# Residual of two tiles moved from VectorE to TensorE and ScalarE, and a down product cut into two column blocks

## The chip, the cores and the metric

The kernel runs on one core of a Trainium2 chip. The metric is the device time of one execution in microseconds, the median of several runs; less is better. The profile's span, from first to last instruction, is 1.7 to 1.8 us shorter than the time of the same execution.

Names used below: PE is TensorE, DVE is VectorE, ACT is ScalarE, POOL is GpSimd, SP is SyncE. A tile is 128 of the 2048 tokens.

## The reference, cut to what matters

```python
# x: (1, 2048, 448); H = 16 heads of 28; F = 1792
x = A_x
h = x + A_ref(layernorm(x))        # linear attention: softmax features, num / den, then @ wo
h2 = h + B_ref(layernorm(h))       # (sigmoid(hn @ w_gate) * (hn @ w_up)) @ w_down
```

`num / den` is the normalisation of the attention output, tile by tile. `h = x + (o @ wo)` is the first residual; its row sums start the second layer norm. The last step multiplies with `w_down` and adds `h`.

## The kernel before

Every operation is recorded in a graph with what it reads and writes; `ORDER` fixes each engine's queue, and waits between engines are derived from the graph. So a change consists of operations and of new queue orders.

```python
def num(t):                        # attention output of tile t, then its normalisation
    b = {1: 2}.get(t, 6)           # PSUM banks 6 and 7 for every tile but tile 1
    op("pe", "num%d" % t, ...)     # 16 small matmuls
    op("dve", "rsm%d" % t, ...)    # reciprocal
    op("dve", "qq%d" % t, ...)     #   needs rsm
    op("dve", "b%d" % t, ...)      #   needs qq
    op("dve", "c%d" % t, ...)      #   needs b
    op("dve", "den%d" % t, ...)    #   needs c; last reader of the banks: num(t+1) waits for it
    op("dve", "rden%d" % t, ...)
    op(("pool", "dve"), "o%d" % t, ...)
# ...
def resid(t, b):                   # b: the bank that holds o @ wo of tile t
    op("dve", "h%d" % t, ...)      # h = psum + x, with row sums
    op("dve", "nm%d" % t, ...)     # minus mean
    op("act", "sq%d" % t, ...)     # square, with row sums
    op("pool", "ve%d" % t, ...); op("pool", "pow2_%d" % t, ...)
    op("dve", "hn%d" % t, ...)     # normalised h
    # tiles 0 and 1: four PE transposes (hT) and a VectorE copy (hTe); others: a DMA transpose
# ...
def gate_up(t0, n, ff):            # 14 blocks ff; gate and up banks (4,5) for even, (0,1) for odd ff
    op("pe", "ga" + nm, f1, r=hk + wgu_keys, ...)   # waits for the hidden tiles and eight weight loads
    op("pe", "gb" + nm, f2, ...)
    op("act", "sig" + nm, ...)     # tanh of the gate bank
    op("dve", "hh" + nm, ...)      # (tanh + 1) * up, frees the banks
# ...
def finish(t, b):
    op("dve", "fin%d" % t, ...)    # down product * 0.5 + h
    op("sp", "out%d" % t, ..., dma="out", nring=16)
# ... at the end of SyncE's queue:
if e == "sp":
    for sem, v in last_out.items():        # every DMA semaphore: loads, transposes, outputs
        eng.wait_ge(sems[sem], v)
```

`down1` does the down product of tiles 12 to 15, one tile and 448 columns at a time; tile 13 was the last to end. The changed kernel ends with tile 15.

The softmax here doesn't subtract the row's maximum and nothing guards it: scores larger than these inputs give would overflow.

Of the kernel before, what the change touches and what calls it, by code (L numbers as in the profile page):

```python
# [6 lines left out]
ALU = mybir.AluOpType  # L7
# [11 lines left out]
class Graph:  # L19
# [86 lines left out]
    def emit(self, nc):  # L106
# [71 lines left out]
P = 128  # L178
D = 448
H = 16  # L180
# [25 lines left out]
        "x1 x0 ld_k0 x2 ld_k2 x4 x6 ld_v0 x10 ld_v2 x8 ld_q2 ld_q1 ld_q3 x12 ld_q0 xT4 xT5 x14 xT6 xT7 xT8 xT9 xT10 "  # L206
        "xT11 xT12 xT13 xT14 xT15 ld_wg0 ld_wu1 ld_wu3 ld_wd1 ld_wg1 ld_woo1 ld_wg3 ld_woe1 ld_wu0 ld_woe0 ld_wg2 "
        "ld_woo0 ld_wu2 ld_wd6 ld_wd5 oT2 ld_wd2 oT3 oT4 oT5 ld_wd4 oT6 ld_wd3 ld_wd0 oT7 hT2 hT3 hT4 oT8 oT9 hT5 hT6 "
        "hT7 oT11 oT10 oT12 out3 out1 hT9 hT8 oT13 hT11 hT10 oT14 oT15 out5 hT12 hT14 out2 hT15 out4 hT13 out9 out7 "
        "out10 out6 out14 out0 out15 out12 out11 out8 out13 "  # L210
# [4 lines left out]
        "ek10 xn14 ek11 xn15 v1_11 ek12 eq0_0 ek13 v1_13 ek14 v1_14 ek15 v1_15 eq0_1 kvzB eq1_0 eq1_1 eq2_0 oT0e oT1e "  # L215
        "eq2_1 sq0 sq1 eq3_0 eq3_1 sig0_1 sig0_0 sig0_3 sig0_2 sig0_5 sig0_4 sq2 sq3 sig0_7 sig0_6 sig0_9 sig0_8 "
        "sig0_11 sig0_10 sq5 sig0_12 sig0_13 sq4 sq7 sig2_0 sig2_1 sq6 sig2_3 sig2_2 sig2_5 sig2_4 sig2_6 sig2_7 "
        "sig2_8 sig2_9 sig2_10 sig2_11 sig2_12 sig2_13 sig4_1 sq9 sig4_0 sig4_3 sq8 sig4_2 sig4_5 sig4_4 sig4_7 "
        "sig4_6 sig4_9 sq10 sig4_8 sq11 sig4_11 sig4_10 sig4_13 sig4_12 sig8_1 sig8_0 sq13 sig8_2 sig8_3 sig8_4 "
        "sig8_5 sq12 sig8_6 sq14 sq15 sig8_7 sig8_9 sig8_8 sig8_10 sig8_11 sig8_13 sig8_12 sig12_0 sig12_1 sig12_3 "  # L220
        "sig12_2 sig12_5 sig12_4 sig12_7 sig12_6 sig12_8 sig12_9 sig12_11 sig12_10 sig12_12 sig12_13 "
# [3 lines left out]
        "ppa0 warm9 ppb0 vva0 xT3 xT2 vvb0 ppa2 ppb2 vva2 vvb2 kva0 w2m1_1 w2m1_0 pva4 kvb0 pvb4 pva5 kva1 pvb5 kvb1 "  # L225
        "pva6 kva2 pvb6 pva7 w2m1_2 w2m1_3 pvb7 pva8 kvb2 kva3 pvb8 kvb3 pva9 kva4 pvb9 kvb4 pva10 kva5 pvb10 pva11 "
        "kvb5 kva6 pvb11 pqa0_0 pva12 kvb6 kva7 pvb12 kvb7 pqb0_0 kva8 pva13 kvb8 kva9 pvb13 pva14 kvb9 kva10 pvb14 "
        "kvb10 kva11 pva15 kvb11 pvb15 pqa0_1 kva12 pqb0_1 kvb12 kva13 pqa1_0 kvb13 kva14 pqb1_0 kvb14 kva15 kvb15 "
        "pqa1_1 num0 num1 pqb1_1 pqa2_0 pqb2_0 num2 pqa2_1 oT0 pqb2_1 oT1 num3 woa0 wob0 pqa3_0 num4 pqa3_1 pqb3_0 "
        "pqb3_1 num5 hT0 hT1 ga0_1 woa2 gb0_1 ga0_0 num6 gb0_0 ga0_3 wob2 gb0_3 ga0_2 gb0_2 num7 ga0_5 ga0_4 gb0_5 "  # L230
        "gb0_4 woa4 ga0_7 ga0_6 gb0_7 gb0_6 wob4 num8 ga0_9 ga0_8 gb0_9 gb0_8 ga0_11 ga0_10 gb0_11 gb0_10 woa6 num9 "
        "wob6 ga0_13 ga0_12 gb0_13 gb0_12 dn0_0 dn0_4 ga2_0 ga2_1 gb2_0 gb2_1 dn0_8 dn0_11 ga2_3 num10 ga2_2 gb2_3 "
        "dp0_0 gb2_2 dp0_4 ga2_5 ga2_4 gb2_5 gb2_4 dp0_8 dp0_11 ga2_6 ga2_7 gb2_6 gb2_7 woa8 ga2_8 ga2_9 gb2_8 gb2_9 "
# [6 lines left out]
        "dn10_8 ga12_0 ga12_1 gb12_0 dn8_0 dn10_11 gb12_1 ga12_2 dp10_0 ga12_3 dn8_4 gb12_3 gb12_2 dp10_4 dn8_8 "  # L240
        "ga12_5 dn8_11 ga12_4 gb12_5 gb12_4 dp8_0 dp8_4 ga12_7 ga12_6 gb12_7 dp10_8 dp10_11 gb12_6 dp8_8 dp8_11 "
        "ga12_9 ga12_8 gb12_9 gb12_8 dm14_0 dm12_0 dm15_0 ga12_11 ga12_10 gb12_11 gb12_10 dm12_4 dm14_4 dm13_0 "
        "ga12_12 ga12_13 gb12_12 gb12_13 dm15_4 dm14_8 dm15_8 dm12_8 dm15_10 dm14_10 dm14_12 dm14_13 dm15_12 dm12_10 "
        "dm12_12 dm15_13 dm12_13 dm13_4 dm13_8 dm13_10 dm13_12 dm13_13 "
# [3 lines left out]
        "bst10 agg11 bst9 bst7 agg6 agg7 agg9 bst8 agg8 agg10 xT3e xT2e ss0 nm1_8 nm1_6 rs0 ss1 rs1 bst12 bst13 ss2 "  # L248
        "bst14 rs2 agg14 xn8 ss3 agg13 agg12 rs3 xn9 bst15 ss4 agg15 xn10 ve1_12 ss5 rs4 ss6 rs5 ss7 rs6 v1_8 ss8 "
        "v1_9 rs7 ss9 rs8 v1_10 ss10 rs9 rs10 ss11 v1_12 rs11 phi10 ss12 rs12 ss13 rs13 ss14 rs14 ss15 rs15 phi15 "  # L250
        "kvzA kvzD kvzC rsm0 qq0 b0 rsm1 c0 qq1 den0 b1 rden0 c1 rsm2 den1 qq2 rden1 b2 c2 den2 rden2 rsm3 qq3 b3 c3 "
        "den3 rden3 h0 nm0 h1 rsm4 nm1 qq4 b4 c4 den4 hn0 hn1 rsm5 hT0e hT1e rden4 qq5 b5 c5 den5 rden5 hh0_1 rsm6 "
        "qq6 b6 hh0_0 c6 h2 den6 hh0_3 rden6 hh0_2 rsm7 h3 qq7 nm3 nm2 b7 hh0_5 hh0_4 c7 den7 rden7 o7 hh0_7 hh0_6 "
        "hn2 rsm8 hn3 qq8 h4 hh0_9 hh0_8 b8 h5 c8 den8 hh0_10 nm4 hh0_11 nm5 rsm9 h6 qq9 h7 b9 c9 hh0_12 hh0_13 nm7 "
        "rden8 nm6 den9 hh2_0 hh2_1 hn4 rsm10 rden9 qq10 b10 hh2_3 c10 hh2_2 hn6 hn7 den10 hh2_5 hh2_4 fin0 fin1 "
        "hh2_6 hh2_7 hn5 rden10 hh2_8 hh2_9 h8 h9 hh2_10 hh2_11 rsm11 qq11 nm9 b11 hh2_13 c11 hh2_12 den11 rsm12 qq12 "
        "nm8 b12 c12 rden11 hh4_1 hh4_0 o10 den12 hh4_3 rsm13 qq13 b13 rden12 hh4_2 c13 hh4_5 den13 fin3 hn9 rden13 "
        "hh4_4 hn8 fin2 rsm14 hh4_7 o13 qq14 b14 c14 hh4_6 den14 h10 h11 nm10 hh4_9 nm11 rsm15 hn10 hh4_8 hn11 hh4_11 "
        "qq15 h13 h12 hh4_10 b15 c15 hh4_13 nm13 hh4_12 den15 nm12 rden15 o15 rden14 hh8_1 hh8_0 o14 hh8_2 hh8_3 fin4 "
        "fin5 hh8_4 hh8_5 h15 h14 nm14 hh8_6 nm15 hn12 hn14 hh8_7 hh8_9 hh8_8 hn13 hn15 hh8_11 hh8_10 hh8_12 hh8_13 "  # L260
        "fin6 fin7 hh12_0 hh12_1 hh12_3 hh12_2 hh12_5 hh12_4 hh12_7 fin11 hh12_6 fin9 fin10 fin8 hh12_8 hh12_9 "
        "hh12_11 hh12_10 hh12_12 hh12_13 fin14 fin15 fin12 fin13 "
# [3 lines left out]
        "pow1_2 nb1_3 ve1_4 nm1_4 pow1_4 nb1_2 nb1_4 xn2 mask2 opad0 ve1_6 pow1_6 ve1_8 v1ones pow1_8 nb1_6 phi0 "  # L266
        "nb1_8 xn7 phi1 phi2 phi3 nm1_12 pow1_12 nb1_12 phi4 phi5 phi6 phi7 phi8 phi9 phi11 phi12 phi13 phi14 kvzones "
        "o0 o1 o2 o3 ve0 pow2_0 ve1 pow2_1 o4 o5 o6 ve2 pow2_2 ve3 pow2_3 ve5 ve4 pow2_4 o8 pow2_5 ve7 o9 ve6 pow2_7 "
        "pow2_6 ve8 ve9 o11 pow2_9 o12 pow2_8 ve10 pow2_10 ve11 pow2_11 ve12 pow2_12 ve14 pow2_14 ve15 ve13 pow2_15 "
        "pow2_13 "  # L270
# [3 lines left out]
    "pq:0,0,4 pq:0,1,4 kvz pq:1,0,0 pq:1,1,4 pq:2,0,0 num:0 num:1 ot:0 ot:1 wo:0 pq:2,1,4 pq:3,0,0 num:2 num:3 "  # L274
    "wo:2 pq:3,1,4 gu:0,2 num:4 num:5 wo:4 gu:2,2 num:6 num:7 wo:6 down:0,2 num:8 num:9 wo:8 down:2,2 num:10 "
    "num:11 wo:10 gu:4,4 num:12 num:13 wo:12 down:4,2 num:14 num:15 wo:14 down:6,2 gu:8,4 down:8,2 down:10,6 "
    "gu:12,4 down1:12,2 down1:13,3 down1:14,6 down1:15,7 "
# [31 lines left out]
def build(nc, A_x, A_wqkv, A_w_phi, A_wo, B_w_gate, B_w_up, B_w_down, out):  # L309
# [8 lines left out]
    NX, NO, NH, NPHI, NS, NE, NV, NSG, NHH = 3, 4, 3, 3, 3, 5, 5, 4, 2  # L318

    with ExitStack() as es:  # L320
# [99 lines left out]
        def kvzones(e):  # L420
            e.tensor_copy(kvz[:, 0:2, :, :].rearrange("p a g (h e) -> p a g h e", e=E)[:, :, :, :, E - 1],
                          maskK[:, :, :, 0][:, :, None, :].to_broadcast([P, 2, G, 2]))
            return e.tensor_tensor(kvz[:, 2, :, :].rearrange("p g (h e) -> p g h e", e=E)[:, :, :, E - 1],
                                   maskK[:, 0, :, 0][:, None, :].to_broadcast([P, G, 2]),
                                   maskK[:, 1, :, 0][:, None, :].to_broadcast([P, G, 2]), ALU.add)

        op("pool", "kvzones", kvzones, r=["maskK"], w=KVZ)


# [255 lines left out]
        def num(t):  # L685
            s, c = t % NS, t // 4
            b = {1: 2}.get(t, 6)

            def f(e):
                def part(half, x):  # L690
                    return [(bk(b + x)[:, (sg * G + gg) * 2 * E:(sg * G + gg + 1) * 2 * E], eq[c][half, sg, gg, TS(t)],
                             kvz[half, x if sg == x else 2, gg, :], True, True) for sg in range(2) for gg in range(G)]
                return both(e, part(QL, 0), part(QH, 1))
            op("pe", "num%d" % t, f, r=[("eq", c, i) for i in range(2)] + KVZ, w=[B(b), B(b + 1)], rows=64,
               half={b: 0, b + 1: 1})
            ov = psum[:, b * 512:(b + 2) * 512].rearrange("p (a n) -> p a n", a=2)
            OPv = ov[:, :, 0:8 * E].rearrange("p a (h e) -> p a h e", e=E)
            OMv = ov[:, :, 8 * E:16 * E].rearrange("p a (h e) -> p a h e", e=E)
            BB = [B(b), B(b + 1)]

            def h2(ap):
                return ap[:, s, :].rearrange("p (a h) -> p a h", a=2)

            def h3(ap):
                return ap[:, s, :, :].rearrange("p (a h) e -> p a h e", a=2)
# [20 lines left out]
            if t >= 2:  # L726
                otrans(t)
# [36 lines left out]
        def wout(t):  # L764
            def ot(t):
                return lambda h, k: oT[h, t % NO, k, :]
# [84 lines left out]
        for step in PROGRAM.split():  # L851
# [19 lines left out]
            elif k == "down1":  # L871
                down1(v[0], v[1], late)
# [37 lines left out]
```

## Time and profile before

| | before |
|---|---|
| time, three runs | 207.3 us (206.97 to 207.31) |
| span | 205.35 us |
| PE busy | 196.1 us, 96% |
| PE idle between 50 and 72 us | 1.8 us |
| after the last matmul | 4.4 us |

The prediction below shows the lines and how to read them: which engine is full, where TensorE is not, and what each of its gaps waited for. One view the prediction quotes only in words. The source view of SyncE's final waits in the kernel before (line, engine, operation, count, shortest/median/longest duration in ns, first and last start in us):

```profile
L174 SPq EVENT_SEMAPHORE  x48: 17/28/28, 202.0 to 204.9; - x48
```

48 wait instructions in 2.9 us stand between the last output's issue and the end.

### The profile page before, as it was taken

The numbers are of one execution on the slowest core, as the hardware profiler recorded it, in microseconds if no ns is written. First come the engines' busy times: TensorE is split into PE (matmuls) and PEld (weight loads), VectorE is DVE, ScalarE is ACT, GpSimd is POOL, SyncE is SP. The second block draws the span as 40 slices with busy tenths as digits, with TensorE's granted clock in tenths as the row PEclk, the third lists the DMA queues.
The fourth block names the chain that finished last, engine by engine and source line by source line (L and its number), as shares of the span: only waits on it lengthen the run. The fifth ranks groups of instructions, "written<-read, shape, count | busy, mean of one in ns | idle before, by whom it ended". The sixth has DMA issues, their size and how long they took to land.

```text
span 205.4 us, 5793 instructions
## 1 busy us (share of the span) xinstructions
PE 196.1 (96%) x2456; PEld 108.7 (53%) x2456; DVE 135.8 (66%) x341; ACT 96.2 (47%) x189; POOL 60.4 (29%) x101
## 2 busy tenths in 40 slices
PE   7899999989989999999999999999999999999991
PEld 2745556655566676676444444445555545544450
DVE  5899999879899996776758886356232523353151
ACT  2889999879782636222342532335322122132100
POOL 4699998963443304400041110001400000000000
PEclk9999999999999999999999999999999999999999
DMA  5975653999314630412006311110321000020013
GB/s 151 314 139 121 81 80 54 330 287 282 96 30 96 144 56 0 80 34 46 3 0 123 78 30 25 30 26 24 78 51 26 0 0 3 0 89 3 0 40 117
DMA packets 32722, 16.25 MB, mean 79 GB/s; under 512 B 24952, under 2 KB 31800, under 8 KB 32696
## 3 DMA queue, kind: packets, MB, share of 16 engines
q1 hardware_dynamic: 32192, 15.86, 33.2%
q8 instruction: 19, 0.31, 0.6%
q10 hardware_dynamic: 504, 0.03, 0.2%
q14 instruction: 7, 0.06, 0.1%
HBM read 8.34 MB, written 1.84 MB: 50 GB/s over the span
## 4 chain that ended last, share of the span: by engine, by line
PE 88%; DVE 7%; DMA 1%; issue 1%; ACT 0%; POOL 0%; DVEq 0%
PE psum L292 82%; PE psum L836 5%; DVE st L493 2%; DMA x_sb<-in_A_x_dram 1%; PE psum L561 1%; DVE b_sb L709 1%; DVE c_sb L712 1%; PE psum L486 1%; DVE kvz L677 1%; DVE x_sb L740 1%; DVE xnT L479 0%; DVE mv L494 0%; DVE hn_pad L754 0%; DVE x_sb L843 0%; DVE rsm L706 0%
## 5 line engine op out<-in xcount | busy, mean ns | idle before, releaser
L292 PE MATMUL psum<-xnT,wg_sb 64*128 64x512 bf16 (+1 forms) x490 | 94.3, 334 | 1.2 <-DVE hhT L810 0.6
L292 PE MATMUL psum<-xnT,wu_sb 64*128 64x512 bf16 (+1 forms) x490 | 94.3, 334 | 0.1
L809 ACT ACTIVATE sg_sb<-psum 128x512 bf16<-128x512 f32 (+1 forms) x70 | 34.9, 511 | 88.6 <-PE psum L292 88.0
L810 DVE SCALAR_TENSOR_TENSOR hhT<-sg_sb,psum 128x512 bf16<-128x512 bf16 (+1 forms) x70 | 39.1, 577 | 50.9 <-ACT sg_sb L809 50.3
L292 PEld LDWEIGHTS psum<-xnT,wg_sb 64*128 64x128 bf16 x490 | 43.9, 94 | 24.6 <-DVE hhT L810 5.8
L292 PEld LDWEIGHTS psum<-xnT,wu_sb 64*128 64x128 bf16 x490 | 43.9, 94 | 14.2 <-PE psum L292 0.3
L292 PE MATMUL psum<-wd_sb,hhT 64*128 64x448 bf16 x336 | 37.2, 349 | 0.0
L292 PEld LDWEIGHTS psum<-wd_sb,hhT 64*128 64x128 bf16 x336 | 17.0, 94 | 15.0 <-DVE x_sb L740 0.6
L616 POOL TENSOR_TENSOR phi<-hhT,rs 128x896 bf16<-128x896 bf16 x14 | 24.0, 1735 | 0.9 <-PE psum L292 0.8
L292 PE MATMUL psum<-Wk,xnT 64*128 64x448 bf16 x112 | 22.3, 350 | 0.3
L292 PE MATMUL psum<-wv_sb,xnT 64*128 64x448 bf16 x112 | 22.4, 351 | 0.1
L748 POOL TENSOR_SCALAR ve<-ssq 128x1 f32<-128x1 f32 x16 | 3.4, 215 | 64.5 <-ACT junk L745 64.0
L612 DVE TENSOR_REDUCE ss<-hhT 128x32 f32<-128x896 bf16 x16 | 17.0, 1062 | 0.7 <-ACT hhT L609 0.6
L292 PE MATMUL psum<-xnT,Wq 64*120 64x512 bf16 x112 | 14.7, 383 | 0.1
L722 POOL TENSOR_TENSOR o_pad<-c_sb,rden 128x448 bf16<-128x448 bf16 x11 | 10.3, 936 | 14.6 <-DVE rden L717 12.7
L292 PE MATMUL psum<-wo_e,oT 64*128 64x448 bf16 x56 | 13.2, 350 | 0.3 <-ACT oT L479 0.3
L292 PE MATMUL psum<-wo_o,oT 64*128 64x448 bf16 x56 | 13.2, 350 | 0.1
L745 ACT ACTIVATE junk<-x_sb,nm 128x448 bf16<-128x448 bf16 x16 | 10.6, 663 | 2.7 <-DVE nm L743 2.7
L843 DVE SCALAR_TENSOR_TENSOR x_sb<-psum,x_sb 128x448 bf16<-128x448 f32 x16 | 9.4, 619 | 3.5 <-PE psum L836 3.1
L836 PE MATMUL psum<-wd_sb,hhT 128*128 128x448 bf16 x56 | 11.1, 353 | 0.0
L292 PEld LDWEIGHTS psum<-Wk,xnT 64*128 64x128 bf16 x112 | 7.6, 94 | 5.4 <-ACT hhT L609 0.7
L493 DVE BATCH_NORM_STATS2 st<-x_sb 128x6 f32<-128x448 bf16 x16 | 9.3, 609 | 1.6 <-DMA x_sb<-in_A_x_dram 1.5
(82 smaller groups left out, 238.0 us busy)
## 6 DMA issues: line engine op xcount, KB each, us to landing
out_dram<-x_sb SPq DMA_DIRECT2D x16, 112.0 KB, 1.8
x_sb<-in_A_x_dram SPq DMA_DIRECT2D x7, 224.0 KB, 4.5
wd_sb<-in_B_w_down_dram SPq DMA_DIRECT2D x7, 224.0 KB, 4.4
wg_sb<-in_B_w_gate_dram SPq DMA_DIRECT2D x3, 448.0 KB, 7.9
wu_sb<-in_B_w_up_dram SPq DMA_DIRECT2D x3, 448.0 KB, 7.0
wv_sb<-in_A_wqkv_dram SPq DMA_DIRECT2D x2, 224.0 KB, 5.0
wk_sb<-in_A_wqkv_dram SPq DMA_DIRECT2D x2, 196.0 KB, 3.7
wo_e<-in_A_wo_dram SPq DMA_DIRECT2D x1, 336.0 KB, 9.0
```

The costliest lines, as they stand in the source:

```text
L292: p = e.matmul(o, lhsT=w, rhs=r, start=st, stop=sp, tile_position=(row, 0))
L486: p = e.transpose(ps[:, kt * P:(kt + 1) * P], src, ident[:])
L493: op("dve", "bst%d" % t, lambda e: e.bn_stats(st1[:, t, :], x_sb[:, t, :]), r=[("x", t)], w=[("st1", t)])
L612: op("dve", "ss%d" % t, lambda e: e.tensor_reduce(ss[:, s, :], eks, AX.X, ALU.add), r=[("ek", s)], w=[("ss", s)])
L616: return e.tensor_tensor(phi[:, sp, :, :, :].rearrange("p b a n -> p (b a) n")[:, :, 0:56].rearrange("p b (h d) -> p b h d", h=2), eks.rea ...
L722: return e.tensor_tensor(o_pad[:, so, off:off + D].rearrange("p (h d) -> p h d", h=H), c_sb[:, s, :, 0:DH], rden[:, s, :][:, :, None].to_b ...
L745: op("act", "sq%d" % t, lambda e: e.activation(junk[:, t % 2, :], h_sb[:, t, :], ACT.Square, bias=nm2[:, t:t + 1], accum_out=ssq2[:, t:t + ...
L748: op("pool", "ve%d" % t, lambda e: e.tensor_scalar(ve2[:, t:t + 1], ssq2[:, t:t + 1], 1.0 / D, EPS, op0=ALU.mult, op1=ALU.add), r=[("ssq2" ...
L809: op("act", "sig" + nm, lambda e: e.activation(sg_sb[:, k, 0:N], bk(bg)[:, 0:N], ACT.Tanh, scale=0.5), r=[B(bg)], w=[("sg", k)])
L810: op("dve", "hh" + nm, lambda e: e.scalar_tensor_tensor(out=hhT[(t0 // 4) % NHH][:, ff, ns], in0=sg_sb[:, k, 0:N], scalar=1.0, in1=bk(bu)[ ...
L836: p = e.matmul(bk(b)[:, 0:D], lhsT=hb[:, ff, TS(t)], rhs=wd_sb[:, ff, :], start=ff == 0, stop=ff == FT - 1)
L843: op("dve", "fin%d" % t, lambda e: e.scalar_tensor_tensor(out=h_sb[:, t, :], in0=bk(b)[:, 0:D], scalar=0.5, in1=h_sb[:, t, :], op0=ALU.mul ...
```

## The change

Its intent: VectorE is over 90% busy between 50 and 72 us, so the first two tiles' residual is added by identity matmuls into the same PSUM bank as the projection, and evacuated on ScalarE with row sums. The last tile's down product is cut into 320 and 128 columns, so that only a small evacuation and a small output follow the last matmul. With this come a copy (oT1) moved from ScalarE to VectorE, o7 moved to POOL (and o8 and o9, later on, from POOL to VectorE), a fourth buffer for the normalisation, mask columns moved from POOL to ScalarE, and new queue orders on all engines. The core of the diff:

```diff
-        def resid(t, b):
+        def resid(t, b, ha=False):
+            if ha:
+                op("act", "h%d" % t, lambda e: e.activation(h_sb[:, t, :], bk(b)[:, 0:D], ACT.Identity, accum_out=sum2[:, t:t + 1]), ...)
+            else:
                 op("dve", "h%d" % t, ...)
@@ def wout(t):
+            ha = t in (0,)
+            def xp(t, b, h, first):
+                return [(bk(b)[:, 0:D], ident[h, :], x_sb[h, t, :], first, False)] if ha else []
-                return both(e, [(bk(2)...
+                return both(e, xp(t, 2, LO, True) + [(bk(2)...
@@ def down1
-        def down1(t, b, parts):
+        def down1(t, b, parts, w=0):
+            for nm, b, lo, hi in (("dm", b, 0, D - w), ("dl", 4, D - w, D))[:1 + (w > 0)]:
+                ...                       # matmuls, evacuation and output of columns lo to hi
@@ PROGRAM
-    "... down1:14,6 down1:15,7 "
+    "... down1:14,6 down1:15,7,128 "
@@ ORDER, "sp": the weight loads
-  ld_wg0 ld_wu1 ld_wu3 ld_wd1 ld_wg1 ld_woo1 ld_wg3 ld_woe1 ld_wu0 ld_woe0 ld_wg2 ld_woo0 ld_wu2 ld_wd6 ld_wd5 oT2 ...
+  ld_wg0 ld_wu1 ld_wu3 ld_wd1 ld_wg1 ld_woe0 ld_wu0 ld_woe1 ld_woo0 ld_woo1 ld_wg3 ld_wg2 ld_wd6 ld_wd2 ... ld_wu2 oT2 ...
@@ ORDER, "dve": the first tiles
-  ... den3 rden3 h0 nm0 h1 rsm4 nm1 qq4 b4 c4 den4 hn0 hn1 rsm5 hT0e hT1e rden4 qq5 b5 c5 den5 rden5 hh0_1 ...
+  ... den2 oT1e rsm3 ... rden2 rden3 rsm4 nm1 qq4 b4 nm0 c4 den4 rden4 hn1 rsm5 qq5 b5 hn0 c5 hT1e den5 hT0e rden5 ...
@@ ORDER, "pe": the first gate/up blocks
-  ... num5 hT0 hT1 ga0_1 woa2 gb0_1 ga0_0 num6 gb0_0 ga0_3 wob2 ... ga0_9 ga0_8 gb0_9 gb0_8 ga0_11 ...
+  ... num5 pqb3_1 hT1 hT0 num6 ga0_1 ga0_0 gb0_1 gb0_0 woa2 num7 ... ga0_9 ga0_8 gb0_9 gb0_8 woa6 ga0_11 ...
```

## The prediction

> **What bounds the kernel now.** I read the page first, then the chain of work that ended last, then busy time by stretch, then the timelines of TensorE, VectorE and ScalarE between 50 and 72 us, and last the final 10 us. The page's part 1:
>
> ```profile
> PE 196.1 (96%) x2456; PEld 108.7 (53%) x2456; DVE 135.8 (66%) x341; ACT 96.2 (47%) x189; POOL 60.4 (29%) x101
> ```
>
> TensorE is busy 96% of a 205.4 us span, so 9.3 us without a matmul is all there is to win unless matmul work goes away. Busy time by stretch (us, then PE, PEld, DVE, ACT, POOL busy with counts) says where those 9.3 us lie:
>
> ```profile
> 50.00:60.00 10.00, 8.82 (x127) 4.99 (x125) 9.19 (x31) 8.71 (x14) 4.97 (x9) 1.00 0.40 97
> 60.00:72.00 12.00, 11.36 (x208) 8.03 (x204) 11.27 (x39) 5.67 (x15) 4.17 (x7) 1.00 0.48 104
> 72.00:183.00 111.00, 110.95 (x1298) 60.36 (x1300) 64.83 (x163) 36.01 (x78) 12.24 (x28) 1.00 0.17 34
> 201.00:205.40 4.40, 0.00 (x0) 0.00 (x0) 0.62 (x1) 0.00 (x0) 0.00 (x0) 1.00 0.30 102
> ```
>
> From 72 to 183 us TensorE loses 0.05 us: nothing the change does there can matter except through the matmul count. Idle time sits in 50 to 72 (1.18 + 0.64 = 1.8 us), in the last 4.4 us, and before 50, where the change barely reaches. In 50 to 72 VectorE is at 92% and 94%: this is the one long stretch where TensorE is fed by a full VectorE. The chain of waits for 50 to 60 us agrees: from 52.23 to 59.28 it runs on VectorE through num3's and num4's normalisation, h0, h1, the two layer-norm outputs and the transposes' copies. TensorE's own rows (start, us, what, idle before and releaser):
>
> ```profile
> 52.53 0.36 PE L292 MATMUL psum<-wo_e,oT 64*128 64x448 bf16 x1 [0.34 <-ACT oT L479]
> 57.74 0.40 PE L292 MATMUL psum<-kvz,eq 56*128 56x60 bf16 x16 [0.19 <-DVE den L714]
> 59.37 0.27 PE L292 MATMUL psum<-xnT,wg_sb 64*128 64x256 bf16 x1 [0.58 <-DVE xnT L479]
> 72.04 0.28 PE L292 MATMUL psum<-xnT,wg_sb 64*128 64x256 bf16 x1 [0.61 <-DVE hhT L810]
> ```
>
> These four gaps add up to 1.72 us. The first is the wait for the copy of oT1, the third for the normalised first tiles; the last is a bank being freed: gb0_9 ends, tanh 0.38 us, product 0.42 us, and no other matmul had been placed between.
>
> The VectorE work that the change takes away, and the end of the kernel:
>
> ```profile
> 54.46 0.56 DVE L740 SCALAR_TENSOR_TENSOR x_sb<-psum,x_sb 128x448 bf16<-128x448 f32 x1
> 55.13 0.62 DVE L740 SCALAR_TENSOR_TENSOR x_sb<-psum,x_sb 128x448 bf16<-128x448 f32 x1
> 200.99 0.63 DVE L843 SCALAR_TENSOR_TENSOR x_sb<-psum,x_sb 128x448 bf16<-128x448 f32 x1 [0.92 <-PE psum L836]
> ```
>
> **What the Trainium skill says.** "TensorE: Matmul & The Clock Gate", Back-to-back issue gap, gives N/2.4 + 2.5 ns between isolated warm matmuls: 189 ns for 448 columns. The trace agrees: the output projection's pairs start at 52.73, 52.92, 53.11. "ScalarE: Activation LUTs", What ACT_TABLE_LOAD costs, gives 186 ns + 0.833 ns per element with immediate operands (an estimate of 559 ns for 448), about 93 ns more with a pointer bias; the trace has 0.54 us for a 448 copy from PSUM and 0.66 to 0.67 us for the Square with bias, which is followed by a 0.19 us accumulator read. "PSUM — Partial Sum Buffer", The four PSUM rules, says that a nonzero seed for an accumulation should go through TensorE as an identity matmul, or be added after evacuation; the change goes from the second form to the first. No run yet shows its cost. "VectorE: DVE Perf Modes", The TRN2 errata, gives (120 + FD)/0.96 ns for a PSUM source: 592 ns at 448; the trace has 0.56 to 0.63 us.
>
> **The change part by part.**
>
> *Residual of tiles 0 and 1.* It removes h0 and h1 from VectorE: from 54.46 to the next operation at 55.06 is 0.60, from 55.13 to 55.67 another 0.54, so 1.14 us. It adds four half-array identity matmuls of 448 columns, two concurrent pairs at 0.19: 0.38 us of TensorE, all inside the chain from oT1 to the residual. On ScalarE it adds two evacuations with an accumulator: starts of such a copy lie 0.43 us apart (rows at 40.46 and 40.88), plus about 0.16 for the read, 0.6 each, so 1.2 us. Before, h on VectorE and the squares on ScalarE overlapped; now h1, h0, sq1, sq0 follow each other on one engine.
>
> *oT1's copy goes from ScalarE to VectorE.* It costs VectorE 0.38 (the two hT copies take 0.76). Before, oT1 was ready at 51.85, the copy ended at about 52.48, the projection started at 52.53. VectorE is free at 51.7 once rden2 is put later, so I expect the projection at 52.34: 0.2 us earlier.
>
> *o7 moves to POOL* (VectorE minus 0.55), and the mask columns go from POOL to ScalarE. The latter ended at 44.17 before and the masks waited for matmuls until 44.62, so it gives nothing. VectorE's balance up to 72 us: -1.14 + 0.38 - 0.55 = -1.3 us.
>
> *The order.* Every pair of gate/up blocks of the first half chunk now has a filler behind it; woa6 stands where the 0.61 gap was. That gap's true cost is 71.16 to 72.04 less the 0.11 pitch, 0.77 us.
>
> *Last tile in blocks of 320 and 128.* 14 matmuls at 0.190 become 14 at about 0.137 and 14 at about 0.060 (the 128-column transposes start 0.06 apart): 2.66 becomes 2.76, +0.10. The last evacuation shrinks from 0.63 to an estimated 0.29 (a 256-column one takes 0.41, a 512 one 0.69, so 1.1 ns per column): -0.34. What comes after is fixed: the last output is issued at 201.64 and lands at 203.32, but SyncE then runs 48 wait instructions, first at 202.0, last at 204.9, about 61 ns each. The landing is hidden beneath them, so a smaller last transfer gains nothing by being small; one more output semaphore adds up to 0.06. Tail: +0.10 - 0.34 + 0.06 = -0.18 us.
>
> *The middle, walked through by hand.* Projection from 52.34 over nine pairs instead of seven to results at 54.45. ScalarE: h1 from 54.5, h0 55.1, sq1 55.7, sq0 56.4 to 57.15; POOL's two small steps take 0.8 each: scales at 57.3 and 58.1. VectorE interleaves num4 and num5: hn1 57.35, hn0 58.8 (it stands after b5 in the queue), hT1 copied at 60.2, hT0 at 60.75. Gate/up then starts near 60.8 instead of 59.37, with num6 (0.24) already done. That is 1.2 us late, 0.38 of it the added matmuls. Then it is given back: the projection of tiles 2 and 3 no longer lies between the first gate/up blocks, VectorE's load is lower, and the 0.77 gap closes. At ga0_13, where both orders have done the same work, I get 75.5 against 75.14: +0.36 us. My walk is conservative with VectorE (I let it idle about 1.2 us in all), so the true value may lie a microsecond lower.
>
> **The rivals.**
> 1. *VectorE was the limit and the relief comes through* (for: 92 to 94% busy where TensorE waits; against: num to normalisation to num is a round trip that fewer operations only turn into idle time). The middle gains 1.3 - 0.38 = 0.9 us, the tail 0.2: 206.2.
> 2. *ScalarE's serial chain takes VectorE's place* (for: ScalarE is at 8.71 of 10 us in 50 to 60 and the q exponentials that free banks 4 and 5 come after; my walk). Middle +0.36, tail -0.18: 207.5.
> 3. *Late loads*: one up-weight load moves behind five down-weight loads. It landed at 52.7; five loads of 224 KB at the 280 to 330 GB/s of that stretch take 3.4 to 4 us and put it near 56.5, still before 59. Nothing; if it came in late, 208.5.
> 4. *The tail gains more*, if the landing and not SyncE's waits were the limit: another 0.3. The landing 1.6 us before the last wait speaks against it.
>
> **Range and chances.** I give rival 1 somewhat more weight than my walk, as the new order was evidently arranged around the freed VectorE: 0.55 x 206.2 + 0.4 x 207.5 + 0.05 x 208.5 = 206.8. The range takes in both with a few tenths for the runs' own spread (206.97 to 207.31): 205.6 to 208.1. Faster by 2% would need 203.1, thus 4.1 us, when the gaps in reach total 1.8 plus about 0.3 of tail: 2 in 100. Slower by 2% would need a new stall of 4 us: 2 in 100.
>
> **What would show it right or wrong.** Right: two VectorE rows of L740's kind fewer, two ScalarE evacuations of 448 with accumulator reads at about 54.5; the two output-projection groups still at 56 matmuls each, and 4 more with the identity; projection start near 52.3; no gap of 0.6 near 72; last evacuation near 0.29 us, then the same row of waits on SyncE. Wrong: gate/up starting before 59.5 would mean that my chain of h1, h0, sq1, sq0 is too pessimistic, and the time goes to 206 or under; a gap before it above 2 us, or TensorE waiting for the q exponentials at its second gate/up block, puts it above 207.5. A tail after the last matmul other than about 4.1 us would say that SyncE's waits are not what follows it.

## The result, and the profile after

| | before | after |
|---|---|---|
| median of 4 runs, us | 207.31 (206.97 to 207.35) | 207.04 (206.96 to 207.22) |
| ratio, 95% interval | | 0.9992 (0.9975 to 1.0009) |

A ratio here is the mean time of one kernel's runs over the mean of the other's in the same rounds, so it is not quite the ratio of the medians. The interval spans 1: the change did not move the time by anything these runs can tell from zero.

The page's part 1 and then busy time by stretch of the changed kernel (columns as in the prediction):

```profile
PE 197.3 (96%) x2474; PEld 113.2 (55%) x2474; DVE 135.7 (66%) x340; ACT 97.3 (47%) x195; POOL 57.9 (28%) x98
```

```profile
50.00:60.00 10.00, 8.95 (x122) 4.49 (x118) 8.81 (x30) 9.04 (x17) 4.67 (x8) 1.00 0.63 161
60.00:72.00 12.00, 11.24 (x226) 9.53 (x228) 11.34 (x38) 5.12 (x14) 5.01 (x8) 1.00 0.30 59
72.00:183.00 111.00, 110.95 (x1288) 62.10 (x1286) 65.00 (x165) 36.76 (x80) 10.65 (x27) 1.00 0.19 35
201.00:205.50 4.50, 0.34 (x7) 0.17 (x3) 0.44 (x2) 0.00 (x0) 0.00 (x0) 0.95 0.24 77
```

TensorE is idle 1.05 + 0.76 = 1.8 us between 50 and 72 us, the same sum as before. Only its place has changed. TensorE's rows in the timeline (start, us, what, and in brackets idle time before and releaser):

```profile
52.60 0.36 PE L291 MATMUL psum<-x_sb,ident 64*128 64x448 bf16 x2 [0.18 <-DVE oT L480]
...
59.47 0.40 PE L487 MATMUL psum<-ident,hn_pad 128*128 128x128 bf16 x4 [0.60 <-DVE hn_pad L760]
60.43 0.40 PE L291 MATMUL psum<-kvz,eq 56*128 56x60 bf16 x16 [0.57 <-DVE den L717]
61.03 0.27 PE L291 MATMUL psum<-xnT,wg_sb 64*128 64x256 bf16 x1 [0.20 <-ACT eq L648]
```

The 0.34 us before the projection is now 0.18 us and the 0.61 us gap near 72 us is gone. In their place come 0.60 us before tile 0's transposes (they now follow tile 1's), 0.57 before num6, and 0.20 before gate/up, which starts at 61.03 instead of 59.37. The four gaps add up to 1.55 us against 1.72.

ScalarE's rows of the new residual, from its timeline:

```profile
54.75 0.54 ACT L743 ACTIVATE x_sb<-psum 128x448 bf16<-128x448 f32 x1 [0.95 <-PE psum L291]
55.31 0.20 ACT L743 ACTIVATION_READ_ACCUMULATOR x_sb<-psum 128x1 f32 x1
55.42 0.53 ACT L743 ACTIVATE x_sb<-psum 128x448 bf16<-128x448 f32 x1
...
55.93 0.66 ACT L751 ACTIVATE junk<-x_sb,nm 128x448 bf16<-128x448 bf16 x1
...
57.24 1.00 ACT L647 ACTIVATE eq<-psum 120x1024 bf16<-120x1024 f32 x1
```

h1, h0, sq1 and sq0 run back to back from 54.75 to the next exponential at 57.24. The end of the kernel, from the timeline and from the source view of SyncE's final waits:

```profile
201.38 0.29 DVE L854 SCALAR_TENSOR_TENSOR x_sb<-psum,x_sb 128x128 bf16<-128x128 f32 x1 [0.23 <-PE psum L847]
```

```profile
L174 SPq EVENT_SEMAPHORE  x48: 27/28/28, 202.1 to 205.0; - x48
```

The evacuation fell from 0.63 to 0.29 us, and the row of 48 waits is still there.

To see where the time went I cut both traces at the same events, taken as starts in TensorE's timeline. "Projection" is tile 0's output projection, identity matmul included. "Block 13" is ga0_13, the first of the last pair of the first half chunk; by then both kernels have done the same operations on TensorE, whatever their order, but for the identity matmuls.

| stretch, us | before | after | difference |
|---|---|---|---|
| start to num0 | 46.00 | 46.22 | +0.22 |
| num0 to projection | 6.53 | 6.37 | -0.16 |
| projection to first gate/up | 6.84 | 8.43 | +1.59 |
| first gate/up to block 13 | 15.77 | 14.40 | -1.37 |
| block 13 to end of last matmul | 125.81 | 125.91 | +0.10 |
| last matmul to end of span | 4.40 | 4.12 | -0.28 |
| span | 205.35 | 205.46 | +0.11 |

The first row is not told apart from scatter: num0 stood between 45.95 and 46.68 us in all the profiles, in both orders. Without it the change is worth -0.12 us. The two large rows in the middle nearly cancel: +0.22 us together (+0.23 from the stretch 22.61 and 22.84 as tabled below; the difference is rounding).

What became of VectorE's relief is seen in busy time between projection and block 13, of the kernel before and then of the changed one (length, then PE, PEld, DVE, ACT, POOL):

```profile
52.53:75.14 22.61, 21.09 (x356) 14.20 (x358) 21.48 (x72) 12.75 (x27) 7.47 (x13) 1.00 0.42 90
```

```profile
52.60:75.43 22.83, 21.16 (x360) 15.04 (x361) 20.37 (x71) 13.74 (x32) 8.69 (x15) 1.00 0.36 74
```

VectorE lost 21.48 - 20.37 = 1.11 us of work, and its idle time rose from 1.13 to 2.46 us. The freed time became idle time. TensorE's idle time went from 1.52 to 1.67 us. Where this happened is seen when the stretch is cut at the first gate/up block, before:

```profile
52.53:59.37 6.84, 6.00 (x83) 3.38 (x83) 6.54 (x23) 5.71 (x9) 2.80 (x6) 1.00 0.34 77
59.37:75.14 15.77, 15.09 (x274) 10.82 (x276) 14.94 (x51) 7.04 (x19) 4.66 (x7) 1.00 0.45 96
```

and after:

```profile
52.60:61.03 8.43, 6.94 (x103) 3.61 (x103) 7.58 (x26) 7.42 (x14) 3.40 (x7) 1.00 0.41 84
61.03:75.43 14.40, 14.23 (x258) 11.43 (x259) 12.79 (x46) 6.32 (x18) 5.28 (x9) 1.00 0.34 68
```

Ahead of gate/up VectorE got more work, 7.58 us instead of 6.54: its new queue holds qq5, b5, c5 and den5 ahead of and between the two copies that gate/up waits for (hT1e and hT0e); before, they stood behind them. TensorE's idle time there rose from 0.84 to 1.49 us. The relief lies behind the start of gate/up (14.94 to 12.79 us), where TensorE is idle for only 0.17 us of 14.40 and little more can be won. Of VectorE's 2.46 us of idle time 1.61 are there. Of the other 0.85, VectorE waits 0.22 us for num4 and 0.30 us for ScalarE's h1, both before 55.54 us; from then to gate/up no gap of VectorE is longer than 0.06 us.

The new order did let the normalisations run ahead: num9 starts at 70.58 us instead of 74.33. But no matmul had been short of that tile.

### The profile page after: what moved, and what is told of

Its sections match the earlier page's. It is cut to its first block, busy times and chain, and to the rows that moved or that the text cites. A ratio compares the mean times of both kernels' runs of the same rounds, so it can differ in the third digit from the quotient of the medians.

```text
span 205.5 us, 5834 instructions
## 1 busy us (share of the span) xinstructions
PE 197.3 (96%) x2474; PEld 113.2 (55%) x2474; DVE 135.7 (66%) x340; ACT 97.3 (47%) x195; POOL 57.9 (28%) x98
## 4 chain that ended last, share of the span: by engine, by line
PE 91%; ACT 4%; DVE 2%; issue 0%
PE psum L291 81%; PE psum L847 5%; PE psum L473 3%; PE psum L487 1%; ACT eq L648 1%; ACT eq L647 1%; PE psum L562 1%; ACT Wk L480 1%; ACT junk L751 1%; ACT x_sb L743 1%; DVE kvz L678 1%; PE psum L549 1%; DVE b_sb L712 0%; DVE c_sb L715 0%; DVE oT L480 0%
## 5 line engine op out<-in xcount | busy, mean ns | idle before, releaser
L291 PE MATMUL psum<-xnT,wu_sb 64*128 64x512 bf16 (+1 forms) x490 | 92.9, 333 | 0.0
L291 PEld LDWEIGHTS psum<-wd_sb,hhT 64*128 64x128 bf16 x336 | 17.6, 94 | 14.5 <-DVE x_sb L746 0.6
L724 POOL TENSOR_TENSOR o_pad<-c_sb,rden 128x448 bf16<-128x448 bf16 x10 | 9.3, 937 | 15.6 <-DVE rden L720 13.4
L847 PE MATMUL psum<-wd_sb,hhT 128*128 128x448 bf16 (+2 forms) x70 | 11.1, 316 | 0.0
L854 DVE SCALAR_TENSOR_TENSOR x_sb<-psum,x_sb 128x448 bf16<-128x448 f32 (+2 forms) x17 | 9.4, 591 | 2.1 <-PE psum L847 1.6
```

The source lines that it names most:

```text
L291: p = e.matmul(o, lhsT=w, rhs=r, start=st, stop=sp, tile_position=(row, 0))
L724: return e.tensor_tensor(o_pad[:, t % NO, off:off + D].rearrange("p (h d) -> p h d", h=H), c_sb[:, t % NS, :, 0:DH], rden[:, t % NS, :][:, ...
L847: p = e.matmul(bk(b)[:, lo:hi], lhsT=hb[:, ff, TS(t)], rhs=wd_sb[:, ff, lo:hi], start=ff == 0, stop=ff == FT - 1)
L854: op("dve", "fin%d%s" % (t, nm), lambda e: e.scalar_tensor_tensor(out=h_sb[:, t, lo:hi], in0=bk(b)[:, lo:hi], scalar=0.5, in1=h_sb[:, t, l ...
```

## The experiments

For each run the medians are given with those of the kernel before from the same chip. The stretches are from its profile: "num0 to projection", "projection to gate/up", "projection to block 13", "block 13 to last matmul", "tail" (end of last matmul to end of span). The same stretch repeats within some hundredths from profile to profile of kernels that do the same in it (block 13 to last matmul 125.79 to 125.82 in the four profiles without the block split), but for a single TensorE stop of about 0.4 us that fell into some profiles at different places. So stretches can tell apart what the times, with intervals of 0.3 us and more, cannot.

| run | median us | before, same rounds | ratio (95%) | num0 to proj. | proj. to gate/up | proj. to block 13 | tail |
|---|---|---|---|---|---|---|---|
| (before) | | | | 6.53 | 6.84 | 22.61 | 4.40 |
| (after) | 207.04 | 207.31 | 0.9992 (0.9975 to 1.0009) | 6.37 | 8.43 | 22.84 | 4.12 |
| tail_only | 207.56 | 207.41 | 1.0003 (0.9985 to 1.0021) | 7.03 | 6.75 | 22.55 | 4.12 |
| after_no_tail | 207.29 | 207.41 | 0.9999 (0.9979 to 1.0019) | 6.38 | 8.46 | 22.88 | 4.40 |
| h_on_dve | 207.29 | 207.41 | 0.9990 (0.9975 to 1.0005) | 6.37 | 8.60 | 23.02 | 4.13 |
| after_outwaits | 205.60 | 207.41 | 0.9911 (0.9894 to 0.9928) | 6.37 | 8.43 | 22.84 | 2.34 |
| early_waits | 207.03 | 207.48 | 0.9979 (0.9960 to 0.9998) | 6.37 | 8.26 | 22.67 | 4.13 |
| ln_first | 208.04 | 207.48 | 1.0026 (1.0010 to 1.0043) | 6.37 | 7.93 | 23.60 | 4.12 |
| h_split | 207.44 | 207.48 | 0.9994 (0.9979 to 1.0009) | 6.37 | 8.51 | 22.92 | 4.13 |
| split_ln_first | 207.85 | 207.48 | 1.0019 (0.9999 to 1.0039) | 6.37 | 7.87 | 23.45 | 4.13 |
| before_outwaits | 206.20 | 207.38 | 0.9932 (0.9909 to 0.9955) | 7.10 | 6.75 | 22.53 | 2.98 |
| best | 205.20 | 207.38 | 0.9890 (0.9869 to 0.9911) | 6.37 | 8.26 | 22.67 | 2.34 |
| skip_b5 | 206.57 (one run, wrong) | 207.38 | | 6.37 | 7.98 | 22.42 | 4.12 |
| loads_only | 207.41 | 207.29 | 0.9985 (0.9940 to 1.0030) | 6.53 | 6.83 | 22.61 | 4.40 |

The record marks all results as correct. It does so for skip_b5 too, which leaves out a product on purpose, so this mark proves nothing for that run.

### The end of the kernel: tail_only, after_no_tail, after_outwaits, before_outwaits

**tail_only**: the kernel before with the block split alone.

```diff
-    "... down1:15,7 "
+    "... down1:15,7,128 "        # with the new down1, finish and the changed queue tails
```

> The kernel before with only the last part of the change: tile 15 in blocks of 320 and 128 columns, in the changed kernel's order from the last gate/up blocks on. Theory (the end is set by the last evacuation and then by SyncE's row of waits): the stretch from the end of the last matmul to the end of the span goes from 4.40 us to about 4.1, the matmuls grow by 0.1, so the time falls by 0.1 to 0.3 us. Rival (the last output's transfer sets the end): a smaller transfer lands earlier and the time falls by 0.5 us or more.

The tail went from 4.40 to 4.12 us, as expected. The time did not show it (1.0003, an interval of 0.36%): the same profile lost 0.41 us in a stop between block 13 and the last matmul (126.22 us instead of 125.81), and 0.50 us before the projection. From TensorE's timeline:

```profile
52.97 0.35 PE L230 MATMUL psum<-wo_e,oT 64*128 64x448 bf16 x1 [0.83 <-ACT oT L417]
```

The row names ScalarE's copy of oT, but that copy had ended at 52.42. At 52.77 the last output-projection weight landed: a wait for several semaphores is put down to one name. loads_only below takes this up.

**after_no_tail**: the changed kernel without the split.

```diff
-    "... down1:15,7,128 "
+    "... down1:15,7 "
```

> The changed kernel with tile 15 in one block again. Theory: all of the small gain is the tail's, so this one equals the kernel before within 0.2 us, and its tail after the last matmul is 4.4 us again. Rival (the residual on TensorE and ScalarE gains and the tail does not): it stays at the changed kernel's time, 0.2 us or more under the kernel before.

Its tail is 4.40 us again and its time is that of the kernel before within the noise (0.9999). The rest of its profile is the changed kernel's. The split is therefore worth 0.28 us of tail less what its matmuls cost more. That shows in the changed kernel's groups by shape, in the three shapes of the down product (count, busy us, mean ns), where each 448-column matmul of the last tile has become one of 320 and one of 128:

```profile
L847 PE MATMUL psum<-wd_sb,hhT 128*128 128x448 bf16 x42 | 8.6, 353 | 0.0
L847 PE MATMUL psum<-wd_sb,hhT 128*128 128x320 bf16 x14 | 2.4, 300 | 0.0
L847 PE MATMUL psum<-wd_sb,hhT 128*128 128x128 bf16 x14 | 0.9, 219 | 0.0
```

These means overlap. From start to start it is 0.189 us for 448 columns, 0.136 for 320 and 0.056 for 128, so 14 of them went from 2.65 to 2.69 us: 0.04 us more, not 0.10. Block 13 to the last matmul agrees: at most 125.82 us without the split, 125.83 or 125.84 in five of the profiles with it; the changed kernel's own 125.91 is 0.07 above these.

**after_outwaits** and **before_outwaits**: the changed kernel, and the kernel before, with SyncE's last waits cut to the outputs. The loads' and transposes' data have been waited for by the engines that used them.

```diff
-    for sem, v in last_out.items():
+    for sem, v in [(k, x) for k, x in last_out.items() if k[0] == "out"]:
         eng.wait_ge(sems[sem], v)
```

> The changed kernel where SyncE, at the end, waits only for the output DMAs' semaphores (17) and not for those of the loads and transposes, whose data other engines have waited for already. Theory (SyncE's 48 wait instructions of about 61 ns, 202.1 to 205.0, hide the last landing at 203.2): the end moves to the last landing, some 1.7 us earlier, 205.3 us in all. Rival (the end is set by the landing or by what follows it anyway): no change.

> The kernel before with SyncE's final waits on the 16 output semaphores alone. Theory: its end moves to the last landing too, whose transfer is the larger one: tail after the last matmul about 2.85 us (4.40 before; landing at 2.37 after the last matmul plus the 0.48 that the changed kernel with short waits needed after its landing), so about 1.5 us under the kernel before, and the two-block tail, which brought 0.28 us of tail under the long waits, is worth about 0.5 us of tail here. Rival (the waits cost the same whatever the transfer): the tail shortens by the same 1.8 us as in the changed kernel.

In the changed kernel the source view now has 8 rows instead of 48:

```profile
L174 SPq EVENT_SEMAPHORE  x8: 28/28/28, 202.9 to 204.0; - x8
```

The tail fell from 4.12 to 2.34 us, and the time is 0.9% under that of the kernel before. The last output lands at 203.97 and the last wait begins at 203.99: now the landing sets the end. In the kernel before the tail fell from 4.40 to 2.98 us (2.85 was expected), and there the tail is 0.64 us longer than with the small last output, where under the long waits the split had brought 0.28. Of these 0.64, 0.34 are the larger evacuation, 0.18 the time from issue to landing (1.68 us against 1.50), and 0.12 two wait instructions that stand behind the last landing only in the kernel before. So the theory holds with both kernels: SyncE's bookkeeping hid the landing, and the smaller transfer could not pay, by these 0.18 us, until that was gone.

### The middle: h_on_dve, h_split, early_waits, ln_first, split_ln_first, skip_b5

The chain of waits of the changed kernel, in order of time (start, us, what), seems to tell what holds the middle:

```profile
55.31 0.73 ACT x_sb L743 x3
56.03 1.30 ACT junk L751 x4
57.34 0.91 ACT eq L647
...
60.07 0.92 ACT eq L648
60.99 0.04 issue
61.03 2.71 PE psum L291 x52
```

By this, the residual's evacuations on ScalarE push the squares and the exponentials back, and these hold gate/up. This was my second rival in the prediction. The experiments contradict it.

**h_on_dve**: the residual back on VectorE, all else as changed.

```diff
-            ha = t in (0,)
+            ha = False
# ScalarE's queue: h1 h0 taken out;  VectorE's: rden3 h1 rsm4 nm1 h0 qq4 nm0 b4 c4
```

> The changed kernel with the residual of tiles 0 and 1 added on VectorE again (no identity matmuls, no ScalarE evacuations; h1 and h0 set behind rden3 and rsm4 in VectorE's queue), the rest as changed. Theory 1 (VectorE's freed time became idle time, because a ScalarE chain h1, h0, sq1, sq0 took its place): the time stays within 0.5 us of the changed kernel's, VectorE's idle time between the output projection of tile 0 and the thirteenth gate/up block falls from 2.5 to about 1.3 us, and the q exponentials end about 0.9 us earlier. Theory 2 (the residual on the other engines does pay and the new order alone costs): the time rises by 0.8 us or more.

```profile
52.48:75.50 23.02, 21.12 (x358) 14.79 (x358) 21.09 (x75) 12.76 (x28) 8.66 (x15) 1.00 0.38 72
```

VectorE's work is back to 21.09 us, and the stretch is only 0.18 us longer than the changed kernel's 22.84. So some 0.7 us of VectorE's time in this stretch was worth 0.18 us: the residual's move by itself is worth about that, and the rest of the reordering costs more than it. This does not show that VectorE was free: before gate/up its idle time fell from 0.85 to 0.32 us, so most of the work filled its waits for num4 and h1. Nor do the identity matmuls blur the comparison: num4 starts 1.95 us after the projection's start with them and 1.93 without, where TensorE waits 0.19 us for den3 instead. Time: 207.29 against 207.41 of the kernel before, not told apart. The detail of my expectation was off: VectorE's idle time fell to 1.93 us and not 1.3, and the exponentials ended 8.13 us after the start of the projection instead of 8.38, 0.25 and not 0.9 us sooner. They were sooner, though, and gate/up started later (8.60). That speaks against the exponentials as the limit.

**h_split**: one residual on each engine, so that ScalarE's chain is one evacuation shorter.

```diff
+            hb = {2: False, 3: ha}             # identity and ScalarE for tile 1 only
-            resid(t, 2, ha)
-            resid(t + 1, 3, ha)
+            resid(t, 2, hb[2])
+            resid(t + 1, 3, hb[3])
# ScalarE: h1 sq0 sq1;  VectorE: h0 nm0 rsm4 nm1 ...;  tile 0 first in the later chains
```

> The changed kernel with only tile 1's residual on TensorE and ScalarE, tile 0's on VectorE, tile 0 first in the chains behind. Theory (h1, h0, sq1, sq0 one after the other on ScalarE are the new wait): the exponentials end about 0.6 us earlier relative to the output projection (8.38 us after its start as changed), and projection to thirteenth gate/up block falls by 0.1 to 0.5 us although VectorE has 0.6 us more work. Rival (VectorE is the limit): it rises by about 0.3 to 0.6 us.

The exponentials ended 8.05 us after the projection's start, 0.33 us sooner than in the changed kernel, and the stretch was 22.92: 0.08 us longer, not 0.1 to 0.5 shorter (after_no_tail, with the changed kernel's middle, gave 22.88). My theory of ScalarE's serial chain fell here. The rival (VectorE as the limit, 0.3 to 0.6 us longer) did not come true either.

**early_waits**: the first gate/up block waits for eight weight loads that nobody has waited for on TensorE before. The source view of TensorE's wait instructions just before gate/up, changed kernel:

```profile
L166 PEldq EVENT_SEMAPHORE  x5: 51/51/51, 60.5 to 60.9; - x5
```

They start 0.11 us apart, after num6, and gate/up starts when they are through, though hT0 has been copied at 60.71. The experiment lets the transpose hT1 wait for the weights instead:

```diff
-    op("pe", name, f, r=["ident", rkey], w=[B(bank)])
+    op("pe", name, f, r=["ident", rkey] + (wgu_keys if name == "hT1" else []), w=[B(bank)])
```

> The changed kernel where the PE transpose hT1 already waits for the gate and up weights (all landed by 56.8 us), so that the first gate/up block need not. Theory (in the changed kernel TensorE runs five wait instructions of about 0.11 us each after num6, 60.49 to 60.97, and starts gate/up only at 61.03 though hT0 was copied at 60.71; the profile's name for this wait, the q exponentials, is the last of the semaphores and not the cause): gate/up starts 0.2 to 0.3 us earlier after the output projection than the changed kernel's 8.43 us. Rival (the q exponentials, done at 60.98, really hold it): 8.43 stays.

Gate/up started 8.26 us after the projection, 0.17 sooner, and 0.13 us before the exponentials had ended (60.98 and 61.11). The program agrees: the first block uses banks 0 and 1, freed by exponentials that in the changed kernel ended at 59.15; the last ones free banks 4 and 5. So the exponentials did not hold it, and the 0.20 us gap that the timeline put down to them was TensorE working through its own wait instructions. The 0.17 us lasted to block 13 (22.67) and to the end. In the kernel before, the same five rows stood in idle time, waiting for the same copies:

```profile
L166 PEldq EVENT_SEMAPHORE  x5: 51/51/491, 58.5 to 59.4; - x5
```

**ln_first**: layer norm first. VectorE's queue copies the transposes ahead of c5.

```diff
# VectorE
-  b5 hn0 c5 hT1e den5 hT0e rden5
+  b5 hn0 hT1e hT0e c5 den5 rden5
# TensorE
-  hT1 hT0 num6 ga0_1 ga0_0 gb0_1
+  hT1 hT0 ga0_1 ga0_0 num6 gb0_1
```

> The changed kernel with two queue orders altered: VectorE copies hT1 and hT0 before the second half of tile 5's normalisation (b5 hn0 hT1e hT0e c5 den5), TensorE runs num6 after the first two gate blocks. Theory (VectorE's queue order, not lack of VectorE, sets the start of gate/up; behind it stands ScalarE's chain): gate/up starts 7.6 to 7.9 us after the output projection (8.43 as changed), then the second gate block waits for the q exponentials at about 61.0, and projection to thirteenth gate/up block falls from 22.84 by 0.1 to 0.4 us. Rival (the later start was given back in full anyway): gate/up starts earlier, and 22.84 stays within 0.1.

Gate/up did start 0.50 us sooner after the projection (7.93). But the stretch became 0.76 us longer (23.60), the worst of all, and the time rose by 0.3%. TensorE's timeline shows the price:

```profile
60.79 0.27 PE L230 MATMUL psum<-xnT,wg_sb 64*128 64x256 bf16 x1 [0.67 <-DVE xnT L419]
64.27 0.40 PE L230 MATMUL psum<-kvz,eq 56*128 56x60 bf16 x16 [0.71 <-DVE den L656]
```

num7 now waits 0.71 us for den6. The first part of my theory held: VectorE's queue order sets the start of gate/up. The rest and the rival were wrong, for the delay came out one round later. num6, put behind two gate blocks, starts 8.89 us after the projection instead of 7.83; VectorE waits 0.56 us for it, and num7 then waits for VectorE. This points to a third theory. Every num but num1 uses banks 6 and 7, so num(t+1) cannot start before den(t), and between them lie rsm, qq, b, c, den, each waiting for the one before. In the changed kernel num3 to num7 start at 52.01, 54.55, 57.45, 60.43 and 63.31: one round takes 2.5 to 3.0 us. By this theory it is a chain in series over TensorE and VectorE; neither engine's load sets it, and whatever is queued into it lengthens it.

**split_ln_first**: both of the above.

> Both: one residual on each engine, and the transposes' copies ahead of c5. Theory: the two waits are in line behind each other, so together they give more than either alone: gate/up starts 7.3 to 7.7 us after the projection, projection to thirteenth block falls to 22.2 to 22.5 (22.84 as changed, 22.61 before). Rival (VectorE the limit): no better than the split alone.

23.45 us, 0.61 us longer than the changed kernel. The gain expected from both together did not come: num7 waits 0.70 us for den6, so the same round is delayed. The rival's words, no better than the split alone, came true, but by this wait.

**skip_b5**: a test of the third theory. The product b5 is left out (tile 5's result is then wrong), so one round of the chain is shorter by one dependent operation, while TensorE and ScalarE keep all their work.

```diff
+            if t != 5:
                 op("dve", "b%d" % t, ...)
```

> Wrong on purpose: the changed kernel without the product b5 of tile 5's normalisation (c5 reads an old buffer), which shortens the serial chain num5 to den5 by about 0.6 us and leaves ScalarE and TensorE their work. Theory (the chain num, normalise, free the banks, next num, with the layer norm's steps queued in it, sets the stretch, not any engine's load): projection to thirteenth gate/up block falls from 22.84 by 0.3 to 0.6 us. Rival (ScalarE's h1, h0, sq1, sq0 and exponentials are the limit): gate/up cannot get ahead of the exponentials, 8.38 us after the projection starts, and it falls by under 0.1 us.

```profile
52.47:74.89 22.42, 21.19 (x361) 14.59 (x362) 19.87 (x70) 13.75 (x32) 8.68 (x15) 1.00 0.34 69
```

The stretch fell by 0.42 us to 22.42, for a row of 0.64 us. Gate/up started 7.98 us after the projection, ahead of the end of the exponentials (60.45 and 60.86). The size is as expected, but TensorE's timeline shows the gain at another place:

```profile
58.34 0.94 PE L426 MATMUL psum<-ident,hn_pad 128*128 128x128 bf16 x8
59.85 0.40 PE L230 MATMUL psum<-kvz,eq 56*128 56x60 bf16 x16 [0.57 <-DVE den L657]
```

The wait for den5, the theory's own, is still 0.57 us. What shrank is the wait of tile 0's transposes, from 0.60 to 0.15 us: they need hn0, which stands right behind b5 in VectorE's queue. So skip_b5 and ln_first, where the copies ahead of c5 and den5 brought gate/up forward by 0.50 us, show that what stands before the copies in VectorE's queue sets the start of gate/up. They do not show that the chain does so rather than VectorE's load: the queue has no gap there, and b5 is both. ln_first shows the ring at work one round later, with VectorE itself waiting. There is one profile of each, and no run here parts the two.

### The loads, and the best version: loads_only, best

**loads_only**: the kernel before with only the changed order of the weight loads, as in the diff above under "sp".

> The kernel before with only the changed kernel's order of the weight loads (the four output-projection weights ahead of the last gate weights and of five down weights). In the profiles with the old order the last of these weights landed at 52.13, 52.77 and 53.13 us and the projection of tile 0 started 6.53, 7.03 and 7.10 us after num0, in the new order always 6.37 (weights landed by 49.2). Theory (the late load is a part of the kernel before's time, in most of its runs): num0 to projection is 6.53 us here, held by ScalarE's copy of oT1 and not by a load, and the time falls by 0.2 to 0.5 us. Rival (the wait is given back by the stretch behind it, as others were): the time stays within 0.1 us of the kernel before.

In the three profiles with the old order the last projection weight landed at 52.13 (before), 52.77 (tail_only) and 53.13 us (before_outwaits), against copies of oT1 that ended at 52.48, 52.42 and 52.70. Here it landed at 49.94 and the stretch from num0 to the projection is 6.53 us, as expected: ScalarE's copy, not a load, releases it. But the time is not told apart: 207.41 against 207.29, ratio 0.9985 (0.9940 to 1.0030). What can be said is that the six runs lie within 207.12 to 207.48, while of the eleven of the kernel before in the same rounds three lie above that: 207.76, 208.43 and 210.1. The gain in the mean, if any, is in those, and stays open: no profile shows what they lost.

**best**: the changed kernel with both finds, after_outwaits and early_waits.

> The changed kernel with both finds: short final waits at SyncE (1.8 us) and the weights' waits moved to hT1 (0.17 us). Theory: they are independent, so about 1.9 us under the changed kernel and 2.0 under the kernel before, 205.3 to 205.5 us, ratio near 0.990. Rival: the 0.17 us is lost in the later stretch and only the 1.8 remain, which these rounds can hardly tell apart, but the profile can: projection to thirteenth gate/up block 22.67 against 22.84 us.

205.20 us, 0.989 of the kernel before, and both parts are in its profile: 22.67 us from projection to block 13, tail 2.34. It beats both kernels, by about 2.2 and 1.8 us in the medians.

## Why the prediction was right or wrong

The measured 207.04 us lies 0.24 us from the number, 206.8, within the range of 205.6 to 208.1, and there was no change of 2%. The nearness is partly luck: 206.8 is in the main a weighted mean of two rivals, 206.2 and 207.5, of which the one with more weight did not happen, and the difference from the kernel before is within the noise. Two figures in the prediction, 189 and 592 ns, are estimates worked out from the formulas of the pages that it names there. Point by point:

- **What bounds the kernel.** Right for 72 to 183 us (0.05 us idle in both). For 50 to 72 us I called it "the one long stretch where TensorE is fed by a full VectorE". That holds up to the start of gate/up: there VectorE is busy for 6.54 of 6.84 us before, and without a gap from 55.54 us on in the changed kernel. Behind it TensorE was idle for only 0.68 us, so there was at most that to win; I took the two as one.
- **Rival 1, the relief comes through, 206.2 us.** This is the step that failed. VectorE's balance was nearly right: -1.3 us predicted, -1.14 measured from num0 to block 13 (27.03 to 25.89 us; oT1's copy lies before the projection). But the middle did not gain 0.9 us: from num0 to block 13 it took 0.07 us longer. Ahead of gate/up VectorE had 1.04 us more to do, and behind it, where 2.15 us were taken away, TensorE's idle time could fall only from 0.68 to 0.17 us. I gave this rival the greater weight, 0.55, because the order was "evidently arranged around the freed VectorE".
- **My walk of the middle, +0.36 us.** No gain was right; the size was 0.07 us (-0.16 and +0.23). I had gate/up at 60.8, hn0 at 58.8 "after b5 in the queue" and hT0 copied at 60.75; measured were 61.03, 59.01 and 60.71, with num0 0.22 us later. The residual began on ScalarE at 54.75 and not 54.5, the projection at 52.60 and not 52.34, both later by about num0's 0.22. The walk's remark that VectorE would idle about 1.2 us was no pessimism; it idled 2.46.
- **Tail, -0.18 us.** The evacuation (0.29 us), the 48 waits and the hidden landing are right; after_outwaits and before_outwaits show the hiding directly. Two terms were not: the matmuls cost 0.04 us and not 0.10, because 128 columns start 0.056 us apart and 320 columns 0.136; and there was no 49th wait, but the issue of the last output took 0.38 us instead of 0.33, which is most of the 0.06. The tail itself went down by 0.28 us.
- **Rival 2, ScalarE's serial chain, 207.5 us.** The traces came near its size (span +0.11 us, +0.18 expected), but not its mechanism. The rows are there, and the chain of waits names them. But h_split and h_on_dve ended the exponentials sooner without gaining, and early_waits started gate/up before they had ended. What the runs show of this chain is VectorE's wait of 0.30 us for h1. In its place stands what is queued on VectorE ahead of the copies (skip_b5, ln_first).
- **The gap near 72 us closes.** Right. It closed by a filler, woa6; the same time came up as gaps before gate/up.
- **Rival 3, late loads.** The up weight landed at 56.76 (56.5 predicted) and did no harm. What I overlooked is the other side of that reorder: the projection's weights had landed only just in time, or too late, and no longer do.
- **What I did not foresee:** the 0.2 us of wait instructions on TensorE before gate/up. They had been hidden by a longer wait.

What stays open: the change's effect on the mean time is below what these runs resolve; how far the projection weights' late landing went into the kernel before's mean; whether ahead of gate/up the serial chain or VectorE's load is the limit; and whether the normalisation chain could be freed with two more PSUM banks, which this layout does not have.

## What to carry to other kernels

Taking work off a busy engine pays only where the bottleneck waits for it: cut the stretch where TensorE's gaps end and read both engines' idle time on each side, and look at what the new order puts in front of the operation that TensorE waits for. Check by the rows, too, that an experiment gained at the place its theory names: skip_b5 gained the expected size at another. A releaser's name in a wait is the last of several semaphores; test it by making that one early before you build on it. And look at what stands between the last result and the end: 40 superfluous wait instructions cost more here than the whole change had to give.

## What the Trainium skill lacked or had wrong

- No page says what a wait instruction in a kernel's queue costs (the nearest is a line on reading a semaphore's value). On SyncE a row of 48 takes 2.9 us, 61 ns each, though the loads and transposes that most of them wait for had landed long before; cutting 40 of them saved 1.78 us of tail. On TensorE's queue five took 0.11 us each. "Perfetto Trace Analysis", Identifying Dependency Chains, says only that such instructions may be inserted.
- "TensorE: Matmul & The Clock Gate", Back-to-back issue gap, gives about 81 ns per matmul for a sustained stream of weight load and matmul at 128 columns, and about 56 ns for an isolated one. Here 14 pairs of weight load and 128-column matmul in a row started 0.055 us apart (200.40 to 201.12 us): the isolated figure held in the stream.
- "ScalarE: Activation LUTs" has the accumulator output but not its cost. Each came with a read row of 0.19 to 0.20 us, and evacuations of 448 columns started 0.67 us apart with it (54.75, 55.42) against 0.43 without.
